# The padding rows of the experts' lists: one DMA of 96 pieces of 512 bytes in place of three of 1024 pieces of 16 bytes

## The chip, the cores and the metric

The kernel runs on one core of a Trainium2 chip. The metric is device time in microseconds (us), from several executions of the same program; a single execution was also taken with the hardware profiler, and all rows below are from that one. The engines are called PE (TensorE; PEld is its weight load), DVE (VectorE), ACT (ScalarE), POOL (GpSimd) and SP (SyncE, which only issues DMAs); SPq and POOLq are their sequencers.

## What is computed

Two stages. The first is attention in two steps: 32 packed queries `p` of each head attend to the 576 keys and values, and the 576 queries `q` then attend to the 32 packed results. The second sends each of the 8 * 576 = 4608 tokens to one of 8 experts (the one with the largest router logit) and scales the expert's output with the softmax weight of that expert.

```
batch, n_heads, seq, head_dim = (8, 8, 576, 64); n_pack = 32
N, D, E, F = (4608, 512, 8, 1024)
p_packed = sm_attn(p, k, v)
out = sm_attn(q, p_packed, p_packed)
...
x = np.ascontiguousarray(attn_out.transpose(0, 2, 1, 3)).reshape(B * S, H * D)
logits = x @ w_gate + modality_bias[modality_id]
e_idx = np.argmax(logits, axis=1)
...
for e in range(E):
    mask = e_idx == e
    h = np.maximum(x[mask] @ w1[e], 0.0)
    out[mask] = gate_w[mask, None] * (h @ w2[e])
```

## The kernel before

Attention goes batch by batch (8 batches). A batch's `k`, `q` and `v` are loaded by SP, each in a DMA of 1152 KB (`load`, line 234); PE transposes them, ACT copies the transposes out of PSUM; PE makes scores, DVE and ACT make the softmax. `xpart` (three steps a batch) makes the attention's output: PE writes a tile of PSUM (`ps<-bd,a2T`, line 366), ACT copies the tokens' values into `xs` (line 371) and the router's logits into `lt` (line 373). `xs` is one tile, not two, so the first copy of a batch waits until the store of the batch before has read it. `xout` (line 377) stores `xs` with one DMA on SP's queue, 1152 KB, into the scratch tensor `x_scr` in DRAM.

The order of all these steps is written out by hand in a string, `ORDER`, for PE, DVE, ACT and SP; POOL is left to the scheduler, which puts its instructions in order of their readiness. Two batches at a time then go through `routing`: `fold` adds up the logits, `bias_all` (the modality's bias) is added on DVE (`lg`, line 440), the largest logit picks the expert, and sums over tokens (`ones_b`, `negtri`) give each token a row in its expert's list.

The lists lie in one DRAM tensor `lst` of E * R = 8 * 4992 rows of four 32-bit words: R is N + PAD, PAD is 384 rows in front of each expert's part, and the tokens' rows follow. A row holds two row numbers in `x_scr`, the row of the output and the gate weight. A token's row is written with an indirect DMA (`scatter`, line 487; 36 of them, 128 rows each). A padding row has 1 << 20 as its output row, which lies outside the output, so that the store at line 887 leaves it out. Blocks of rows are later read back from `lst` (`fetch`, line 754), the tokens gathered from `x_scr` (line 761), and the experts' two matmuls done on them. Up to 200 us the first expert blocks are interleaved with the last batches of attention; from there on only expert blocks run.

The padding rows are written in `routing_consts`, which POOL reaches after the first transposes (`behind` makes its DMAs wait for a copy on ACT). `pad` is a tile in SBUF with E rows of four words in each of its 128 partitions, all the same; a DMA writes one row of each expert from each partition. Behind it in POOL's queue come two more DMAs, `bias2` (`bias` in the rows) and `mid` (the tokens' modalities), and then the instructions that make `bias_all` (lines 126 to 134). The first scatter waits, among others, for the padding's DMAs. Q is 32, P is 128.

Of the kernel before, what the change touches and what calls it, by code (L numbers as in the profile page):

```python
# [11 lines left out]
I32 = mybir.dt.int32  # L12
# [11 lines left out]
def packed_attn_moe_kernel(  # L24
# [14 lines left out]
    nc = tc.nc  # L39
# [3 lines left out]
    E, _, F = w1.shape  # L43
    P = 128
# [8 lines left out]
    PAD = P3  # L53
    Q = P // 4
# [5 lines left out]
    const = ctx.enter_context(tc.tile_pool(name="const", bufs=1))  # L60
# [5 lines left out]
    lst = dram.tile([E * R, 4], I32, name="lst")  # L66
# [24 lines left out]
    meta = const.tile([P, NT, 4], I32, name="meta")  # L91
    metaf = meta.bitcast(F32)
    nc.gpsimd.memset(meta, 0)
    pad = const.tile([P, E, 4], I32, name="pad")
    nc.gpsimd.memset(pad, 0)
    nc.gpsimd.memset(pad[:, :, 1:2], 1 << 20)
    m1 = const.tile([P, NP, NC], F32, name="m1")
# [7 lines left out]
    def behind(ins):  # L105

        tc.add_manual_dep(getattr(ins, "ins", ins), copied[-1].name, SYNC, reason="after the first loads")

    def routing_consts(pool):
        for z in range(0, PAD, P):  # L110
            behind(nc.gpsimd.dma_start(lst.rearrange("(e r) w -> r e w", e=E)[z:z + P], pad))
        mid_d = mod_id.bitcast(I32).rearrange("(i p c w) -> p i (c w)", i=NP, c=NC, w=2)
        mid = sm.tile([P, NP, NC, 2], I32, name="mid", bufs=1)
        bias2 = sm.tile([P, 2, E], F32, name="bias2", bufs=1)
        behind(nc.gpsimd.dma_start(bias2, mod_bias[None].broadcast_to([P, 2, E])))
        behind(nc.gpsimd.dma_start(mid.rearrange("p i c w -> p i (c w)"), mid_d))
        mrow = meta.rearrange("p (i c) w -> p i c w", i=NP)
        for z in range(2):
            nc.gpsimd.iota(mrow[:, :, 5 * z:5 + 4 * z, 1], pattern=[[2 * S, NP], [2, 5 - z]], base=z,
                           channel_multiplier=NC)  # L120
        for z in range(2):
            for u in range(2):
                nc.gpsimd.iota(mrow[64 * u:64 * u + 64, :, :, 3 * z], pattern=[[4 * S, NP], [1, NC]],
                               base=(2 * u + z) * S, channel_multiplier=NC)
        for z in range(2):
            nc.gpsimd.tensor_copy(out=m1[:, :, 5 * z:5 + 4 * z], in_=mid[:, :, z::2, 0])
        m1v = m1.rearrange("p i c -> p (i c)")[:, :, None]
        nc.gpsimd.tensor_scalar(out=m0, in0=m1v, scalar1=-1.0, scalar2=1.0, op0=ALU.mult, op1=ALU.add)
        bias_t = pool.tile([P, NT, E], F32, name="bias_t")
        nc.gpsimd.tensor_tensor(out=bias_all, in0=m0.broadcast_to([P, NT, E]),  # L130
                                in1=bias2[:, 0:1, :].broadcast_to([P, NT, E]), op=ALU.mult)
        nc.gpsimd.tensor_tensor(out=bias_t, in0=m1v.broadcast_to([P, NT, E]),
                                in1=bias2[:, 1:2, :].broadcast_to([P, NT, E]), op=ALU.mult)
        nc.gpsimd.tensor_tensor(out=bias_all, in0=bias_all, in1=bias_t, op=ALU.add)
# [776 lines left out]
    with ExitStack() as actx:  # L911
# [10 lines left out]
        def rest():  # L922
            for m in (4, 8, 12):
                for _ in prep_p(ZL["ps1"], m):
                    pass
                yield
            routing_consts(pzp)
            yield
# [260 lines left out]
```

## Time and profile before

| what | us |
|---|---|
| median of three runs (601.05 to 602.62) | 601.27 |
| the profiled execution, its own time | 601.6 |
| span of the profiled execution, first to last instruction | 599.9 |
| PE busy in it | 558.3 (93%) |
| DVE busy in it | 339.8 (57%) |
| ACT, POOL busy in it | 213.6, 211.0 |

The page cuts the span into 40 slices of 15 us and gives each engine's busy share in tenths. A row of the timeline has the start, the time, the engine, the line, the operation with what it writes and reads, and in brackets how long the engine stood idle before it and which instruction or DMA ended that. A row of the stretches has, for each engine, busy us and the number of instructions, then the granted clock of PE (1.00 is 2.4 GHz, 0.50 is 1.2 GHz), the mean busy share of the 16 DMA engines and what they moved. A DMA's row on an engine is the time of its issue, not of its transfer.

### The profile page before, as it was taken

Reading aid. Unit: us, or ns where it says so; the run is one execution under the profiler, and the core shown is the slowest. Engines: PE = TensorE matmul, PEld = TensorE weight load, DVE = VectorE, ACT = ScalarE, POOL = GpSimd, SP = SyncE. Lnnn points to the kernel's source line nnn. Section 1 sums busy time; section 2 is a strip of 40 time slices with the busy share of each in tenths; the row PEclk is TensorE's granted clock in tenths of the full one; section 3 lists DMA queues with packets and bytes.
Section 4 is the critical chain, followed back from the end, with each engine's and each line's share of the span. In section 5 each row is a group of like instructions: output and inputs, shape, how many; then the busy total and the mean of one; then the engine's idle time right before and its main releaser. Section 6 shows DMA issues by size and latency. Waiting matters only on the chain. (4 is left out here: it accounts for less than half of the span.)

```text
span 599.9 us, 12863 instructions
## 1 busy us (share of the span) xinstructions
PE 558.3 (93%) x4792; PEld 485.4 (81%) x4792; DVE 339.8 (57%) x785; ACT 213.6 (36%) x402; POOL 211.0 (35%) x259
## 2 busy tenths in 40 slices
PE   5999598867799999999999999999999999999994
PEld 4777476745597988988989889898989889989893
DVE  1399497739698717662763436746165375743540
ACT  2587486517443112212213122541222225422230
POOL 4002103651345453445133423164422512741331
PEclk9899799778599999999999999999999999999998
DMA  9799998737233861114551211445211201011331
GB/s 296 240 354 222 348 320 322 222 79 246 91 115 99 194 212 30 61 55 90 141 196 45 70 47 54 99 117 177 74 40 41 86 20 54 37 56 36 54 56 43
DMA packets 33705, 77.09 MB, mean 128 GB/s; under 512 B 7008, under 2 KB 7088, under 8 KB 32576
## 3 DMA queue, kind: packets, MB, share of 16 engines
q1 hardware_dynamic: 24224, 54.92, 29.7%
q0 software_dynamic: 8848, 20.75, 12.3%
q8 instruction: 52, 0.85, 0.6%
q14 instruction: 53, 0.43, 0.3%
q10 hardware_dynamic: 528, 0.13, 0.1%
HBM read 56.53 MB, written 19.26 MB: 126 GB/s over the span
## 5 line engine op out<-in xcount | busy, mean ns | idle before, releaser
L873 PE MATMUL ps_o<-rawq,rawk 128*128 128x512 f32 x460 | 146.8, 390 | 0.0
L837 PE MATMUL ps_h<-x_wide,w1h 128*128 128x256 f32 (+1 forms) x704 | 142.7, 298 | 0.8 <-issue 0.7
L795 DVE STREAM_TRANSPOSE xt<-xt 32x256 f32<-32x256 f32 (+1 forms) x240 | 111.1, 463 | 29.7 <-DMA xt<-x_scr,mt 25.8
L837 PEld LDWEIGHTS ps_h<-x_wide,w1h 128*128 128x128 f32 x704 | 115.0, 189 | 3.3 <-issue 1.7
L761 POOL DMA_INDIRECT xt<-x_scr,mt x82 | 80.6, 983 | 98.5 <-DVE xt L795 30.8
L837 PE MATMUL ps_h<-x_wide,w1l 128*128 128x256 f32 (+1 forms) x352 | 105.3, 299 | 0.7 <-issue 0.7
L873 PEld LDWEIGHTS ps_o<-rawq,rawk 128*128 128x128 f32 x460 | 86.3, 188 | 17.6
L887 POOL DMA_INDIRECT out_dram<-ot,mt x37 | 38.6, 1043 | 122.9 <-ACT ot L879 91.3
L842 DVE SCALAR_TENSOR_TENSOR rawk<-ps_h,rawk 128x256 fp32r<-128x256 f32 (+1 forms) x66 | 29.3, 459 | 86.1 <-ACT rawk L841 72.2
L879 ACT ACTIVATE ot<-ps_o,mt 128x512 f32<-128x512 f32 x35 | 24.1, 689 | 125.6 <-PE ps_o L873 87.9
L837 PEld LDWEIGHTS ps_h<-x_wide,w1l 128*128 128x128 f32 x352 | 66.4, 189 | 0.2 <-issue 0.2
L818 PE MATMUL ps_h<-x_hl,w1h 128*128 128x256 f32 x320 | 58.3, 283 | 1.1 <-issue 1.0
L487 POOL DMA_INDIRECT lst<-meta,dsi x36 | 36.5, 1015 | 52.6 <-DVE nb L268 31.2
L873 PE MATMUL ps_o<-qT,rawk 128*128 128x512 f32 x140 | 54.7, 391 | 0.0
L841 ACT ACTIVATE rawk<-ps_h 128x256 fp32r<-128x256 f32 (+1 forms) x66 | 26.3, 414 | 78.6 <-PE ps_h L837 70.4
L818 PEld LDWEIGHTS ps_h<-x_hl,w1h 128*128 128x128 f32 x320 | 50.0, 189 | 2.0 <-issue 1.5
L818 PE MATMUL ps_h<-x_hl,w1l 128*128 128x256 f32 x160 | 45.3, 284 | 0.1
L299 PE MATMUL ps<-rawv,a1T 64*64 64x128 f32 x576 | 28.4, 308 | 8.8 <-issue 7.1
L873 PE MATMUL ps_o<-rawv,rawk 128*128 128x512 f32 x90 | 35.0, 389 | 0.0
L873 PE MATMUL ps_o<-rawq,x_hl 128*128 128x512 f32 x100 | 34.9, 390 | 0.0
L299 PEld LDWEIGHTS ps<-rawv,a1T 64*64 64x64 f32 x576 | 21.4, 152 | 15.6 <-issue 12.3
L754 POOL DMA_DIRECT2D mt<-lst x19 | 14.9, 782 | 52.3 <-DMA out_dram<-ot,mt 23.8
(234 smaller groups left out, 832.0 us busy)
## 6 DMA issues: line engine op xcount, KB each, us to landing
rawq<-in_q_dram SPq DMA_DIRECT2D x8, 1152.0 KB
rawv<-in_v_dram SPq DMA_DIRECT2D x8, 1152.0 KB
x_scr<-xs SPq DMA_DIRECT2D x8, 1152.0 KB
raw<-in_moe_w_dram SPq DMA_DIRECT2D x32, 256.0 KB
rawk<-in_k_dram SPq DMA_DIRECT2D x7, 1152.0 KB
kT<-in_moe_w_dram SPq DMA_DIRECT2D x4, 1024.0 KB
qT<-in_moe_w_dram SPq DMA_DIRECT2D x3, 1024.0 KB
xt<-x_scr,mt POOLq DMA_INDIRECT x82
```

What stands on the lines that cost most here:

```text
L299: nc.tensor.matmul(pp[u][os_, 0:P], a1T[rs, c, os_], v_t[rs, 2 * pr:2 * pr + 2, TOK[c], :], start=(c == 0), stop=(c == NC - 1), skip_group ...
L487: ins = ins_of(nc.gpsimd.indirect_dma_start(out=lst, out_offset=bass.IndirectOffsetOnAxis(ap=dsi[:, c:c + 1], axis=0), in_=meta[:, i * NC ...
L754: ins = free(nc.gpsimd.dma_start(mt[:, t:], lst[ds(off, rows), :].rearrange("(t p) w -> p t w", p=P)))
L761: return [free(nc.gpsimd.indirect_dma_start(out=xt[:, (t + 2) % 3, u * HW:u * HW + HW], out_offset=None, in_=x_scr[0:NA[ph] * 4 * S] if ph ...
L795: nc.vector.transpose(out=x[w:w + Q, :, z:z + Q], in_=g[z:z + Q, :, w:w + Q])
L818: nc.tensor.matmul(ps[:, f], M[a][:, j, (f0 + f) * P:(f0 + f) * P + P], M["x"][:, j, b, 0:P2], start=(n == 0), stop=(n == 3 * KD - 1))
L837: nc.tensor.matmul(ps, M[a][:, j, f * P:f * P + P], M["x"][:, j, b, cs], start=(n == 0), stop=(n == 3 * KD - 1))
L841: ia = nc.scalar.activation(out=hh, in_=ps, func=AF.Relu)
L842: iv = nc.vector.scalar_tensor_tensor(out=hl, in0=ps, scalar=0.0, in1=hh.bitcast(F32), op0=ALU.max, op1=ALU.subtract)
L873: nc.tensor.matmul(op, hid(M, a, j, 1, slice(t * P, t * P + P))[:, 0], M[b][j // 4][:, j % 4], start=(n == 0), stop=(n == 3 * KF - 1))
L879: ia = nc.scalar.activation(out=ot, in_=op, func=AF.Copy, scale=mt.bitcast(F32)[:, (t + 1) % 3, 2:3])
L887: nc.gpsimd.indirect_dma_start(out=out, out_offset=bass.IndirectOffsetOnAxis(ap=mt[:, (t + 1) % 3, 1:2], axis=0), in_=M["ot"][t == 0], in_ ...
```

## The change

`pad` is made with 12 partitions (PAD // Q) of 32 rows of four words (512 bytes) instead of 128 partitions of 8 rows. One DMA takes the place of the loop of three: from each of the 12 partitions it writes the same 512 bytes to each of the 8 experts, as a run of 32 rows that lie one behind the other in `lst`. What the rows contain, and where they lie, is as before.

```diff
-    pad = const.tile([P, E, 4], I32, name="pad")
+    pad = const.tile([PAD // Q, Q, 4], I32, name="pad")
     nc.gpsimd.memset(pad, 0)
     nc.gpsimd.memset(pad[:, :, 1:2], 1 << 20)
...
     def routing_consts(pool):
-        for z in range(0, PAD, P):
-            behind(nc.gpsimd.dma_start(lst.rearrange("(e r) w -> r e w", e=E)[z:z + P], pad))
+        behind(nc.gpsimd.dma_start(
+            lst.rearrange("(e r) w -> e r w", e=E)[:, 0:PAD].rearrange("e (k r) w -> k e (r w)", r=Q),
+            pad.rearrange("k r w -> k (r w)")[:, None].broadcast_to([PAD // Q, E, 4 * Q])))
```

On PE, DVE, ACT and SP the instructions and their order stay the same. The waits for POOL's DMAs name other semaphores of the same ring of eight, since each later DMA of POOL is now two places earlier in the ring. POOL's queue around the padding before, from the load of the router's weights to the constants that need `mid`:

```order
L1007 DMA wgs<-in_moe_w_gate_dram 64x8x8
L111 DMA lst<-pad 128x8x4 x3
L115 DMA bias_879<-in_moe_modality_bias_dram 128x16
L116 DMA mid<-in_moe_modality_id_dram 128x4x18
L126 CAST m_93<-mid 128x4x5
L126 CAST m_93<-mid 128x4x4
```

The same place after the change (all lines below the new statement are one further down):

```order
L1008 DMA wgs<-in_moe_w_gate_dram 64x8x8
L110 DMA lst<-pad 12x8x128
L116 DMA bias_877<-in_moe_modality_bias_dram 128x16
L117 DMA mid<-in_moe_modality_id_dram 128x4x18
L127 CAST m_93<-mid 128x4x5
L127 CAST m_93<-mid 128x4x4
```

Three DMAs of 128 partitions, 8 experts and 4 words became one of 12 partitions, 8 experts and 128 words; nothing else changed its place.

## Rows read from the trace of the kernel before

**Rows 1.** The page's tenths: PE's busy share in 40 slices of 15 us.

```profile
PE   5999598867799999999999999999999999999994
```

**Rows 2.** Stretches of 4 us: engines' busy us, granted clock, DMA share, GB/s.

```profile
52.00:56.00 4.00, 3.71 (x72) 3.02 (x64) 3.85 (x11) 2.46 (x8) 0.00 (x0) 1.00 1.44 83
56.00:60.00 4.00, 4.00 (x103) 2.50 (x87) 3.52 (x7) 1.95 (x4) 0.00 (x0) 1.00 0.60 94
60.00:64.00 4.00, 0.10 (x14) 0.01 (x2) 1.58 (x3) 0.00 (x0) 0.00 (x0) 1.00 0.96 205
64.00:68.00 4.00, 1.06 (x20) 1.07 (x24) 0.51 (x1) 2.19 (x5) 2.67 (x6) 0.61 1.03 391
68.00:72.00 4.00, 4.00 (x30) 3.64 (x23) 2.23 (x5) 2.83 (x7) 0.00 (x0) 0.54 1.08 401
72.00:76.00 4.00, 4.00 (x117) 3.03 (x114) 2.73 (x8) 2.54 (x5) 0.00 (x0) 1.00 1.00 405
```

**Rows 3.** Waits from 50 to 75 us: who, for whom, total, times, longest.

```profile
ACT xs L371 <- DMA x_scr<-xs: 7.9, 1, 7.9
PE ps L366 <- ACT lt L373: 6.8, 1, 6.8
```

**Rows 4.** Timeline, POOL: start, us, instruction, idle before and its releaser.

```profile
47.70 2.71 POOL L111 DMA_DIRECT2D lst<-pad  x3 [21.09 <-ACT kT L247]
50.40 0.57 POOL L115 DMA_DIRECT2D bias<-n_moe_modality_bias_dram  x1
50.96 0.76 POOL L116 DMA_DIRECT2D mid<-in_moe_modality_id_dram  x1
...
64.73 0.36 POOL L126 CAST m<-mid 128x20 f32<-128x20 int32 x2 [13.01 <-DMA mid<-in_moe_modality_id_dram]
...
66.78 0.79 POOL L134 TENSOR_TENSOR bias_all<-bias_all,bias_t 128x288 f32<-128x288 f32 x1
```

**Rows 5.** Timeline of SP's queue, ACT, DVE and PE around the gap.

```profile
51.20 0.34 SPq L377 DMA_DIRECT2D x_scr<-xs  x1
...
58.94 0.93 PE L366 MATMUL ps<-bd,a2T 64*64 64x136 f32 x24
...
65.81 0.80 ACT L371 COPY xs<-ps 128x768 f32<-128x768 f32 x1 [7.86 <-DMA x_scr<-xs]
...
66.94 1.64 PE L366 MATMUL ps<-bd,a2T 64*64 64x136 f32 x24 [6.83 <-ACT lt L373]
...
67.50 0.75 DVE L348 TENSOR_REDUCE dn<-st 128x18 f32<-128x576 f32 x1 [5.85 <-ACT st L345]
...
68.50 3.50 PE L243 MATMUL ps<-ident,rawq 128*128 128x128 f32 x16
...
72.98 0.23 DVE L440 TENSOR_TENSOR lg<-ps,bias_all 128x72 f32<-128x72 f32 x1 [2.54 <-PE ps L436]
...
76.12 1.09 PE L243 MATMUL ps<-ident,rawq 128*128 128x128 f32 x8
```

**Rows 6.** The stores of `xs`: their size (part 6), and a later one's timeline.

```profile
x_scr<-xs SPq DMA_DIRECT2D x8, 1152.0 KB
...
85.83 0.34 SPq L377 DMA_DIRECT2D x_scr<-xs  x1
...
94.42 0.80 ACT L371 COPY xs<-ps 128x768 f32<-128x768 f32 x1 [0.66 <-PE ps L366]
```

**Rows 7.** Later: a stretch, one group of matmuls, waits 100 to 200 us, scatters.

```profile
200.00:595.00 395.00, 389.33 (x2343) 354.11 (x2342) 202.21 (x437) 105.41 (x193) 149.59 (x149) 1.00 0.29 80
...
73.99 2.20 PE L299 MATMUL ps<-rawv,a1T 64*64 64x128 f32 x72
...
PE ps L299 <- issue: 7.1, 14, 1.0
...
PEld ps L299 <- issue: 11.6, 21, 1.2
...
L487 POOL DMA_INDIRECT lst<-meta,dsi x36: 957/974/1693, 98.8 to 267.2; - x36
```

## The prediction

> **What bounds the kernel now.** I read the tenths of the page first: TensorE is at nine tenths from the twelfth of 40 slices to the last but one, its dips lie in the first third, and after the start the deepest is the fifth slice (60 to 75 us) [rows 1]. From 200 us on it is busy 389.3 of 395.0 us [rows 7], so DMA traffic can give nothing there; but a gain before 200 us moves that whole block forward and is kept. So the question is what the attention stage waits for where this change acts.
>
> The table of stretches shows it. DMA moves 391 to 405 GB/s from 64 to 76 us, but 83 GB/s in 52 to 56 and 94 GB/s in 56 to 60, and in 60 to 64 TensorE works 0.10 us of 4 [rows 2]. The waits name what the engines see: ScalarE's copy of `xs` stood 7.9 us for the DMA `x_scr<-xs`, and TensorE 6.8 us for ScalarE [rows 3]. The timeline gives the order [rows 4, 5]: GpSimd issues the three list-padding DMAs at 47.70 (2.71 us for three), then `bias` at 50.40 and `mid` at 50.96; SyncE issues the first `x_scr<-xs` at 51.20; ScalarE is free at 57.95 (65.81 - 7.86) and starts its next `xs` copy only at 65.81, because `xs` is one buffer that the store still reads; and `mid`, behind the padding in GpSimd's queue, releases its first reader at 64.73, 13.0 us after its issue ended. So what stands behind the padding in its own queue and a store in another queue at the same time are both late by many microseconds, while few bytes move. That is what 3072 pieces of 16 bytes would do, 192 to each of 16 DMA engines. From the end of the first padding DMA's issue (47.70 + 0.9 = 48.6) to 64.73 are 16.1 us, so a piece took at most about 84 ns (an estimate, an upper bound).
>
> **The change part by part.**
>
> 1. *Three DMAs become one.* GpSimd issues for 0.9 us instead of 2.71 [rows 4]. It then idles 13.0 us for `mid` anyway, so these 1.8 us are worth nothing by themselves. The two fills of `pad` stay two fills at the start, smaller: nothing.
>
> 2. *96 pieces of 512 bytes instead of 3072 of 16.* The bytes are the same 48 KB. The trace has no piece of 512 bytes with a price, so I bound it: below by its bytes at the full rate (405 GB/s over 16 engines is 25 GB/s each: 20 ns), above by a small piece plus its bytes (84 + 20 = 104 ns). Six pieces an engine are 0.1 to 0.6 us, against up to 16 before. Either end is far below what follows, so the choice does not matter.
>
> On how they spread there is a rule that speaks against the new form. `pad` now has 12 partitions, and the order of GpSimd's queue, shown with the change, has a DMA of 12 by 8 by 128 words. The Trainium skill, "DMA: Bandwidth & Descriptors", section "Rules for kernel authors", says to put a dimension that is a multiple of 16 outermost, since an outermost size below 16 confines the DMA to at most that many engines; by it 12 engines would carry 8 pieces each and 4 none. No row of this trace has such a DMA.
>
> 3. *The store `x_scr<-xs` at 51.20.* It is 1152 KB [rows 6]. At 391 to 405 GB/s that is 2.9 to 3.0 us after an issue that ends at 51.5: it could land at about 54.5. The other end: the store issued at 85.83 had landed by 94.42, when ScalarE wrote `xs` again and had waited for TensorE, not for the DMA [rows 6]: 8.6 us at most, 59.8 here. ScalarE is free at 57.95, so its wait falls from 7.86 us to between 0 and 1.9. I take 0, because a small rest is covered. TensorE starts its `ps<-bd,a2T` matmuls 1.13 us after the `xs` copy starts (66.94 against 65.81) and is itself busy until 60.11 (66.94 - 6.83): 1.0 us of a rest is hidden. VectorE's `dn` starts 1.69 us after the copy (67.50) and VectorE is busy until 61.65 (67.50 - 5.85): 2.0 us are hidden [rows 5]. At the far end TensorE loses 0.9.
>
> 4. *What comes forward.* TensorE's 6.83 us of idling go. Behind them the granted clock is 0.61 and 0.54 in the stretches 64 to 72, so most of that is at 1.2 GHz instead of 2.4 [rows 2]: the 24 matmuls take 1.64 us where the same group took 0.93 at 58.94, and 16 transposes take 3.50 us where 8 take 1.09 at 76.12 (some 2.1 for 16) [rows 5]. Without the idling I expect the full clock: 0.7 + 1.4 = 2.1 us. TensorE comes forward by 6.83 + 2.1 = 8.9 us. VectorE comes forward by the 5.85 us that it waited for the exponential. The router's logits then reach it at 72.98 - 8.9 = 64.1, before it asks for them (72.98 - 2.54 - 5.85 = 64.6), so the 2.54 us that it waited for them go too: 8.4 us. The least of the two counts: **8.4 us**. If the clock stayed low, the logits would come at 66.15 and VectorE would gain 5.85 + 1.0 = 6.8.
>
> 5. *What is late next.* The q, k and v loads queued behind the store on SyncE's queue run at about 400 GB/s from 64 us to 76. They come forward with the store: store and first q load are 2.36 MB or 5.9 us, so q is there at 58 to 59, and TensorE asks for it at 61. The constants that hang on `mid` are needed by the logits at 64.6 instead of 72.98; they took 2.8 us after `mid` landed (67.57 against 64.73) [rows 4], and `mid` is no longer behind 3072 pieces. The later waits are released by engines or by DMAs that are issued after 64 us, so they move along.
>
> The profiled execution took 601.6 us, with a span of 599.9. 601.6 - 8.4 = 593.2, and the median of the three runs is 0.3 below the profiled one: **592.9 us**.
>
> **The rivals.**
>
> *The new DMA still holds the store.* If the 96 pieces went through one DMA engine, that engine would need 2 to 10 us for them, and its share of the store would end between 56.5 and 64.5. In the middle (60.5) ScalarE waits 2.5 us, TensorE loses 1.5 and VectorE 0.5; TensorE's gain is then the least, 7.4 us: 593.9. At the bad end the wait is 6.5, TensorE loses 5.5 of 8.9 and the time is 597.9. On 12 engines, 8 pieces each are at most 0.8 us, which is hidden as in step 3. By the skill's rule above, the time is thus that of the forecast. For it: an outer size of 12 where the neighbours in the queue have 64 and 128. Against: the pieces lie in 12 partitions, not in one.
>
> *The padding is not what held the store.* `mid` (512 pieces of 72 bytes) and `bias` share the stretch. Then the stall stays: 601.3 us. Against it: `mid` itself is late, which something ahead of it has to explain. Here belongs too that the DMA is cut into 16-byte pieces after all.
>
> *Slower: TensorE runs dry beside the scatters.* 72 matmuls of `ps<-rawv,a1T` take 2.20 us at 73.99, where nothing is scattered. Where GpSimd writes the tokens into the lists (36 scatters, the first at 98.8) the same line has 14 gaps without a releaser, 7.1 us on TensorE and 11.6 us at its weight loads, over two such groups [rows 7]. The cause is not in the trace. If TensorE, which gains 8.9 us where VectorE gains 8.4, met more of the scatters, a third group would cost 3.6 to 5.8 us (half of either sum): 596.5 to 598.7. It is slower than before by over 0.3% only from 8.4 + 1.8 = 10.2 us of new gaps, nearly twice what there is now: 603.1 us or more. For it: the gaps are large and not understood. Against: scatters and matmuls are released from one chain and come forward together.
>
> **How the numbers follow.** Forecast, 590 to 596 (a gain of 5.9 to 8.9 us, and one stretch of low clock, 2.1 us, more or less further on): 0.62. More, below 590, if the later gaps shrink: 0.08. Part lost, 596 to 599.5 (one DMA engine, or a third group of gaps): 0.14. No change, 599.5 to 603.1 (the padding is not the cause): 0.10. Slower, above 603.1: 0.06. About 0.3% (1.8 us) is what a measurement of this kernel can tell from no change; so faster 0.84, same 0.10, slower 0.06. The range from 588 to 598.5 holds the forecast's band, most of the stronger case and most of the weaker one.
>
> **What would show it right or wrong.** Right: no wait of the `xs` copy for `x_scr<-xs`; DMA near 400 GB/s in most of 52 to 60; TensorE busy at full clock from 60 to 68; `mid` released some 5 us after its issue; the first scatter at about 90.4 instead of 98.8. Step 3 is wrong if the `xs` copy still waits over 2 us; step 4 if the first scatter comes forward by much less than 8 us though that wait is gone; step 5 if a wait for q, k, v or `mid` appears before 76 us, or if the time from the first scatter to the end of the span grows.

## The result, and the profile after

| | before | after |
|---|---|---|
| median of six runs each, us | 601.16 | 590.08 |
| range, us | 598.18 to 603.58 | 588.56 to 592.38 |
| profiled execution, span, us | 599.9 | 587.0 |

The ratio is 0.984 with a 95% interval of 0.9807 to 0.9874: a gain of 7.6 to 11.6 us. The medians differ by 11.1 us. (The ratios, here and below, are those given with the measurement; they differ a little from the quotients of the medians, 0.982 here.) The 8.4 us of the forecast lie inside that interval, near its lower end. The profiled execution of after is the fastest of its six (588.56 us), so the two traces lie 13.0 us apart, 2.0 more than the medians.

The stretches of after, with the columns of [rows 2] (busy us of PE, PEld, DVE, ACT, POOL, then the granted clock, DMA share and GB/s):

```profile
52.00:56.00 4.00, 3.62 (x64) 2.91 (x61) 3.85 (x12) 2.44 (x8) 1.87 (x5) 1.00 1.01 316
56.00:60.00 4.00, 4.00 (x87) 2.36 (x84) 3.67 (x7) 3.77 (x8) 1.39 (x2) 1.00 1.01 389
60.00:64.00 4.00, 4.00 (x80) 3.53 (x84) 3.72 (x8) 3.79 (x9) 0.00 (x0) 1.00 1.05 397
64.00:68.00 4.00, 4.00 (x108) 2.93 (x102) 3.80 (x11) 2.73 (x6) 0.00 (x0) 1.00 1.03 412
68.00:72.00 4.00, 4.00 (x50) 3.37 (x48) 3.79 (x13) 3.13 (x5) 0.00 (x0) 1.00 1.04 397
```

The DMA engines now move 316 and 389 GB/s where they moved 83 and 94, PE works 4.00 us of the 4 in which it had worked 0.10, and the granted clock, which fell to 0.61 and 0.54 behind the gap, stays at 1.00.

The timeline of POOL, then SP's queue, ACT, PE and DVE around the place of [rows 4, 5]:

```profile
47.68 0.66 POOL L110 DMA_DIRECT2D lst<-pad  x1 [21.09 <-ACT kT L248]
...
54.03 0.56 POOL L127 CAST m<-mid 128x20 f32<-128x20 int32 x2 [4.31 <-DMA mid<-in_moe_modality_id_dram]
...
90.45 1.13 POOL L488 DMA_INDIRECT lst<-meta,dsi  x1 [32.98 <-ACT lt L374]
...
51.17 0.34 SPq L378 DMA_DIRECT2D x_scr<-xs  x1
...
58.40 0.80 ACT L372 COPY xs<-ps 128x768 f32<-128x768 f32 x1 [0.23 <-ACT kT L248]
...
60.24 0.93 PE L367 MATMUL ps<-bd,a2T 64*64 64x136 f32 x24
61.12 1.97 PE L244 MATMUL ps<-ident,rawq 128*128 128x128 f32 x16
...
61.64 0.75 DVE L349 TENSOR_REDUCE dn<-st 128x18 f32<-128x576 f32 x1
...
64.50 0.19 DVE L441 TENSOR_TENSOR lg<-ps,bias_all 128x72 f32<-128x72 f32 x1
```

Against [rows 5]: the `xs` copy starts at 58.40 instead of 65.81 and has no wait for the store; the matmuls and the transposes behind it run at the full clock (0.93 and 1.97 us for what took 1.64 and 3.50) without a gap; `dn` and `lg` have no idle time ahead of them. The first scatter stands at 90.45 instead of 98.8.

How the gain runs on is seen at a group of the experts' second matmuls (a tile's instructions: duration, then first and last start) and at the last store of the output (timeline). The matmuls of before:

```profile
L873 PE MATMUL ps_o<-rawq,rawk x460: 387/389/477, 206.3 to 590.2; 128*128 128x512 f32 x154
```

The same group of after:

```profile
L874 PE MATMUL ps_o<-rawq,rawk x460: 387/389/476, 196.7 to 579.1; 128*128 128x512 f32 x154
```

The last store of before:

```profile
595.18 1.00 POOL L887 DMA_INDIRECT out_dram<-ot,mt  x1 [6.57 <-POOLq L1150]
```

And of after:

```profile
582.62 1.00 POOL L888 DMA_INDIRECT out_dram<-ot,mt  x1 [5.14 <-POOLq L1151]
```

The lead in these two traces is 8.3 us at the first scatter, 9.6 at 206 us, 11.1 at 590 and 12.6 at the last store.

**Where the cost is recorded.** The DMA view of before from 51 to 65 us (queue, packets, MB, share of the 16 engines' time):

```profile
DMA packets 718, 2.22 MB, mean 159 GB/s; under 512 B 111, under 2 KB 175, under 8 KB 588
...
q1 hardware_dynamic: 556, 2.09, 93.9%
q0 software_dynamic: 160, 0.09, 5.5%
```

The same view of after from 51 to 57 us:

```profile
DMA packets 532, 1.92 MB, mean 321 GB/s; under 512 B 84, under 2 KB 100, under 8 KB 403
...
q1 hardware_dynamic: 435, 1.81, 91.4%
q0 software_dynamic: 96, 0.09, 5.3%
```

q0 is GpSimd's queue with the padding, `bias` and `mid`; q1 carries the store and the loads. The padding does not look guilty: its queue fills 5.5% and 5.3% of the engines' time. The time stands in the records of the other queue, 93.9% for 2.09 MB in 14 us where after needs 91.4% for 1.81 MB in 6. "The DMA engines are 94% busy" says nothing of who holds them; the GB/s beside it shows that they are held. A piece has no record of its own: counted by size in the trace, the padding of before is 48 of q0's 160 packets, 1024 bytes or 64 pieces each, that of after 12 of its 96, 4096 bytes or 8 pieces each. The numbers of pieces below are those of the DMAs' shapes.

### The profile page after: what moved, and what is told of

Same layout as the page of the kernel before. It is cut to its first block, busy times and chain, and to the rows that moved or that the text cites. A ratio compares the mean times of both kernels' runs of the same rounds, so it can differ in the third digit from the quotient of the medians.

```text
span 587.0 us, 12860 instructions
## 1 busy us (share of the span) xinstructions
PE 550.7 (94%) x4792; PEld 478.2 (81%) x4792; DVE 339.7 (58%) x785; ACT 212.7 (36%) x402; POOL 209.2 (36%) x257
## 3 DMA queue, kind: packets, MB, share of 16 engines
q0 software_dynamic: 8784, 20.75, 12.6%
## 5 line engine op out<-in xcount | busy, mean ns | idle before, releaser
L300 PE MATMUL ps<-rawv,a1T 64*64 64x128 f32 x576 | 27.5, 284 | 11.7 <-issue 9.2
L300 PEld LDWEIGHTS ps<-rawv,a1T 64*64 64x64 f32 x576 | 19.9, 138 | 19.4 <-issue 15.1
```

Source lines behind the costliest of these rows:

```text
L300: nc.tensor.matmul(pp[u][os_, 0:P], a1T[rs, c, os_], v_t[rs, 2 * pr:2 * pr + 2, TOK[c], :], start=(c == 0), stop=(c == NC - 1), skip_group ...
```

## The experiments

The runs fell on chips of two kinds: before takes 598 to 601 us on one (the comparison above, the two rows marked 598, and secondxs and earlypad further down) and 575 us on the other. Every ratio is against before on the same chip, with its 95% interval.

| kernel | pieces beside `mid`'s and `bias`'s | first padding issue to first reader of `mid`, us | store's issue to next `xs` copy, us (its wait for the store) | ratio |
|---|---|---|---|---|
| before | 3072 of 16 B | 17.0 | 14.6 (7.9) | |
| after | 96 of 512 B | 6.4 | 7.2 (none) | 0.984 |
| before, 575 us | 3072 of 16 B | 15.7 | 13.3 (6.5) | |
| after, 575 us | 96 of 512 B | 6.1 | (none) | 0.9889 |
| three512 | 96 of 512 B, 3 DMAs | 6.5 | (none) | 0.9894 |
| three512b | the same again | 6.2 | (none) | 0.9902 |
| pieces48 | 1024 of 48 B | 8.8 | 7.6 (0.8) | 0.9898 |
| mixed16 | 1024 of 16 B, 64 of 512 B | 8.4 | 7.6 (0.8) | 0.9922 |
| double16 | 6144 of 16 B | 25.5 | 19.4 (12.4) | 1.015 |
| putback16 (598) | 96 of 512 B, 3072 of 16 B | 19.2 | 15.2 (7.2) | 1.0103 |
| sbuf16 (598) | the same, the 3072 into SBUF | 12.2 | 8.1 (1.4) | 0.9938 |

### Pieces, bytes or DMAs

Three DMAs of 4 partitions by 8 pieces of 512 bytes:

```diff
-        behind(nc.gpsimd.dma_start(
...
+        for z in range(0, PAD // Q, 4):
+            behind(nc.gpsimd.dma_start(
+                lst.rearrange("(e r) w -> e r w", e=E)[:, 0:PAD].rearrange("e (k r) w -> k e (r w)", r=Q)[z:z + 4],
+                pad.rearrange("k r w -> k (r w)")[z:z + 4, None].broadcast_to([4, E, 4 * Q])))
```

> Three DMAs again, but of 32 pieces of 512 bytes each, from 4 partitions each. Theory A (number of small pieces): no wait of the xs copy for the store, 590 us as the changed kernel. Rival B (each DMA costs, or the 1.8 us of issue on GpSimd matter): the wait of 7.9 us is back and the time is 601. Rival C (few engines): 4 partitions could go through 4 DMA engines with 8 pieces each; still no wait.

1024 pieces of 48 bytes (the same bytes, from 128 partitions, in one DMA):

```diff
+    PQ = 3
-    pad = const.tile([PAD // Q, Q, 4], I32, name="pad")
+    pad = const.tile([PAD // PQ, PQ, 4], I32, name="pad")
...
-            lst.rearrange("(e r) w -> e r w", e=E)[:, 0:PAD].rearrange("e (k r) w -> k e (r w)", r=Q),
+            lst.rearrange("(e r) w -> e r w", e=E)[:, 0:PAD].rearrange("e (k r) w -> k e (r w)", r=PQ),
```

> The padding in one DMA of 1024 pieces of 48 bytes from 128 partitions (a third of the pieces of before, the same bytes). Theory A, the store is held by the number of small pieces: in the traces 3072 pieces held it by 65.3 - 56.4 = 9 us, so 1024 hold it by about 3 us; it lands at 59 to 60, the xs copy waits 1 to 2.5 us, TensorE loses 0 to 1.5 us, and the time is 590 to 592. Rival B, the cost is a fixed one for each DMA (three against one): the xs copy waits for nothing and the time is that of the changed kernel, 590.

The first third of the padding in the old form, the rest in the new one:

```diff
+        behind(nc.gpsimd.dma_start(lst.rearrange("(e r) w -> r e w", e=E)[0:P], pad0))
...
-            lst.rearrange("(e r) w -> e r w", e=E)[:, 0:PAD].rearrange("e (k r) w -> k e (r w)", r=Q),
+            lst.rearrange("(e r) w -> e r w", e=E)[:, P:PAD].rearrange("e (k r) w -> k e (r w)", r=Q),
```

> The first 128 padding rows of each expert in one DMA of 1024 pieces of 16 bytes, the other 256 rows in one of 64 pieces of 512 bytes. Theory A (number of small pieces): like 1024 pieces of 48 bytes, the xs copy waits 1 to 2.5 us, 590 to 592 us. Rival B (each DMA costs): two DMAs, half of the stall, 4 us of wait, 594 to 596.

Measured: 569.71, 569.75 and 570.37 us beside 575.09; ratios 0.9894 [0.986, 0.9927], 0.9898 [0.9868, 0.9927] and 0.9922 [0.989, 0.9954]. How long the padding took from issue to landing is the last number in the rows of the DMA issues (KB each, us to landing). three512:

```profile
lst<-pad POOLq DMA_DIRECT2D x3, 16.0 KB, 4.9
```

mixed16, the third in the old form:

```profile
lst<-pad POOLq DMA_DIRECT2D x1, 16.0 KB, 7.6
```

Before, on another 575 us chip (its run is further down):

```profile
lst<-pad POOLq DMA_DIRECT2D x3, 16.0 KB, 11.7
```

And after, on that chip:

```profile
lst<-pad POOLq DMA_DIRECT2D x1, 48.0 KB, 5.0
```

Three DMAs of 512-byte pieces land as soon as one does, so the number of DMAs is not it. All forms write the same 48 KB, and 1024 pieces delay `mid` about alike with all of it (8.8 us) and with 16 KB of it in them (8.4), so the bytes are not it either: the number of small pieces is. No run had many pieces of 512 bytes, so what is due to their number and what to their being small is not separated. A thousand of them are nearly free here: `xs` waits 0.8 us, a little under the 1 to 2.5 us expected and less than the 1.0 and 2.0 us that step 3 had found hidden on PE and DVE, and the three times differ by less than their intervals.

### The 16-byte pieces put back

After, with three DMAs of 1024 pieces into a DRAM tile that nobody reads; then the same number into SBUF; then before with 3072 more into DRAM:

```diff
+            behind(nc.gpsimd.dma_start(dst16[z:z + P, :, 0:4], src16))
```

> The changed kernel with three more DMAs of 1024 pieces of 16 bytes each right behind the new one, from SBUF into a DRAM tensor that nobody reads. Theory A (number of small pieces): the stall of before is back, the xs copy waits 7 to 8 us, mid is late by 8 to 9 us, 600 to 602 us. Rival E, the stall hung on the lists' own addresses (the padding rows lie in eight blocks): no wait, 590.

```diff
+        for z in range(3):
+            behind(nc.gpsimd.dma_start(d16[:, z, :, 0:4], s16))
```

> The changed kernel with three more DMAs of 1024 pieces of 16 bytes each right behind the new one, but from SBUF to SBUF (into the tile for the weights, which is free until 130 us). Theory A in its plain form, every piece costs a DMA engine its time wherever it goes: the stall is back, the xs copy waits 7 to 8 us, 600 to 602 us. Theory A2, it is small writes to DRAM that cost the time: the xs copy waits less than 2 us and the time is 590 to 592.

```diff
         for z in range(0, PAD, P):
             behind(nc.gpsimd.dma_start(lst.rearrange("(e r) w -> r e w", e=E)[z:z + P], pad))
+        for z in range(0, PAD, P):
+            behind(nc.gpsimd.dma_start(dst16[z:z + P, :, 0:4], src16))
```

> The kernel before with 3072 more pieces of 16 bytes, in three more DMAs from another tile to a DRAM tile that nobody reads. Theory (each piece takes its time on the 16 DMA engines; from the first padding issue to the first reader of mid it was 17.0 us with 3072 pieces and 6.4 with 96, so 10.7 us for 3072): mid is released about 27.7 us after the first padding issue, the xs copy waits about 7.9 + 10.7 = 18.6 us, and the time is 10 to 13 us above before. Rival (the stall is a fixed time of a DMA that runs beside the store, or of the write to lst itself, which later readers and the scatters depend on): the wait of the xs copy stays near 8 us and the time near that of before.

The timeline's rows of the `xs` copy and of `mid`'s first reader in putback16:

```profile
65.21 0.80 ACT L377 COPY xs<-ps 128x768 f32<-128x768 f32 x1 [7.24 <-DMA x_scr<-xs]
...
65.75 0.36 POOL L132 CAST m<-mid 128x20 f32<-128x20 int32 x2 [14.58 <-DMA mid<-in_moe_modality_id_dram]
```

In sbuf16:

```profile
60.41 0.80 ACT L376 COPY xs<-ps 128x768 f32<-128x768 f32 x1 [1.35 <-DMA x_scr<-xs]
...
60.99 0.36 POOL L131 CAST m<-mid 128x20 f32<-128x20 int32 x2 [7.57 <-DMA mid<-in_moe_modality_id_dram]
```

In double16:

```profile
69.45 0.80 ACT L376 COPY xs<-ps 128x768 f32<-128x768 f32 x1 [12.44 <-DMA x_scr<-xs]
...
72.01 0.36 POOL L131 CAST m<-mid 128x20 f32<-128x20 int32 x2 [18.84 <-DMA mid<-in_moe_modality_id_dram]
```

putback16 brings the wait of the copy back with data that has nothing to do with the lists, and no gain is left: 601.88 beside 597.87 us, 1.0103 [1.006, 1.0146]. (PE waits 4.6 us behind it, where it waited 5.5 to 6.8 in the two traces of before.) That it is above before, by 4.0 us in the medians, is not explained; its profiled execution was the fastest of four (598.16 to 603.69), and the first scatter stands there at 98.80 us, where it stood in the trace of before (98.78).

double16 gives the price. With 96, 3072 and 6144 small pieces, `mid` comes 6.1, 15.7 and 25.5 us after the first padding issue, all on the same chip: 9.6 and 9.8 us for each 3072. Spread evenly, these are 192 on each of 16 DMA engines, so the price is an estimate of 50 ns a piece and engine (56 on the first pair: 17.03 - 6.35 over 192). `mid`, in the same queue, feels all of it. The store does not: the copy's wait for it grew by 5.9 us, not by the 10.7 expected, and from the store's issue to the next copy it took 13.3 and then 19.4 us. That the store gets a share of the engines while the padding lasts would explain this; it is argued, not shown. The time rose by 9.1 us, to 584.08, 1.015 [1.0101, 1.0199], where 10 to 13 were expected. The first scatter moved back by 5.7 us (96.98 to 102.66), as the wait did; the rest of the 9.1 is not explained, but the interval, 5.8 to 11.4 us, begins close to the 5.7.

sbuf16 changes only where the pieces go: beside the 6.4 us of after, pieces of the same size into SBUF delay `mid` by 5.9 us where those into DRAM (putback16, the same chip) delay it by 12.9. In both, `mid`'s own issue ends 2.6 us later, since GpSimd issues three more DMAs ahead of it; counted from there, its reader waits 7.57 and 14.58 us where it waited 4.31 in after. The `xs` copy waits 1.4 us instead of 7.2. So most of the cost is in the small writes to DRAM. The time is 593.24 us, 0.9938 [0.9912, 0.9964], a little above the 590 to 592 expected; after was not run on that chip. The Trainium skill, "DMA: Bandwidth & Descriptors", section "Why small descriptors are slow (HBM only)", says that transfers inside SBUF don't pay the price of small descriptors; the traces agree in part, since 3072 such pieces still keep `mid` in their own queue waiting 3.3 us longer (7.57 against 4.31).

### Who is hit by the stall

`bias` and `mid` issued ahead of the padding (based on before):

```diff
-        for z in range(0, PAD, P):
-            behind(nc.gpsimd.dma_start(lst.rearrange("(e r) w -> r e w", e=E)[z:z + P], pad))
...
+        for z in range(0, PAD, P):
+            behind(nc.gpsimd.dma_start(lst.rearrange("(e r) w -> r e w", e=E)[z:z + P], pad))
```

> The kernel before, with bias and mid issued ahead of the three padding DMAs instead of behind them. Theory A: mid lands some 4 us after its issue, since nothing is ahead of it, but the store is held as before, the xs copy waits 7 to 8 us and the time is 601. Rival D, the store was held by mid's 512 pieces of 72 bytes: they now run earlier, so the store is held less and the time is 590 to 596.

A second buffer for `xs`, so that the copy need not wait (based on before):

```diff
+            if b == 1 and "xs" not in D_:
+                D_["xs"] = W["raw1"][:, 0:NC * 2 * P].rearrange(
+                    "p (c r d) -> p c r d", c=NC, r=2)
```

> The kernel before, but the second batch's xs lies in another, free tile, so that its copies need not wait for the first store. Theory A: the wait for x_scr<-xs is gone, but the loads behind the store in SyncE's queue are held with it: q lands at 65.7 as before, TensorE asks for it at 61 and waits 4 to 5 us; the gain is 2.5 to 5 us, 596 to 599 us. Rival F, only the one xs buffer made the held store expensive: the whole gain, 590.

The padding issued some 21 us earlier, behind the load of the router's weights (based on before):

```diff
+                        for z_ in range(0, PAD, P):
+                            behind(nc.gpsimd.dma_start(lst.rearrange("(e r) w -> r e w", e=E)[z_:z_ + P], pad))
```

> The kernel before, with the three padding DMAs of 16-byte pieces issued at 26 us, right behind the router's weights, where DMA is idle for some 4 us. Theory A (every transfer beside the small pieces is held): the loads of v and k issued at 27.4 and 28.0 are held by up to 9 us, TensorE waits for k at 34 to 42 us, the store at 51 is free; the time is 592 to 601. Rival G, only the store (a write to DRAM) is held by other writes, loads are not: no wait, 590.

The timeline of midfirst, `mid`'s first reader and the `xs` copy:

```profile
56.55 0.36 POOL L126 CAST m<-mid 128x20 f32<-128x20 int32 x2 [4.55 <-DMA mid<-in_moe_modality_id_dram]
...
65.25 0.80 ACT L371 COPY xs<-ps 128x768 f32<-128x768 f32 x1 [6.54 <-DMA x_scr<-xs]
```

The timeline of secondxs, ACT's copy (into the second buffer, a part of the tile `raw1`), SP's issue of the load of q, and PE's use of it:

```profile
59.40 0.80 ACT L374 COPY raw<-ps 128x768 f32<-128x768 f32 x1 [0.24 <-PE ps L366]
...
52.84 0.38 SPq L234 DMA_DIRECT2D rawq<-in_q_dram  x1
...
66.22 3.26 PE L243 MATMUL ps<-ident,rawq 128*128 128x128 f32 x16 [3.84 <-DVE a2T L356]
```

A wait of earlypad, 26 to 50 us:

```profile
PE ps L297 <- DMA rawv<-in_v_dram: 6.6, 1, 6.6
```

And two stretches of it, with the columns of [rows 2]:

```profile
36.00:40.00 4.00, 1.57 (x25) 0.97 (x9) 3.75 (x11) 3.58 (x8) 0.00 (x0) 1.00 0.86 48
40.00:44.00 4.00, 0.00 (x0) 0.00 (x0) 0.00 (x0) 0.00 (x0) 0.00 (x0) 0.57 0.81 260
```

midfirst frees `mid` early (4.55 us of wait instead of 11.7 to 13.0) and changes nothing for the better: the store still holds the copy 6.54 us (7 to 8 were expected, and in before on the other 575 us chip it is 6.5); 577.29 beside 575.09, 1.0033 [1.0001, 1.0065]. So `mid` was late but not missed.

secondxs takes the copy's wait away and gains nothing in the time: 598.06 beside 597.87, 1.001 [0.998, 1.0039], where 2.5 to 5 us were expected. PE now stands 3.84 us before the transposes of q instead. The profile puts that down to `a2T` on DVE, but in before the same transposes started at 68.50 [rows 5] while that `a2T` started only afterwards:

```profile
69.66 0.78 DVE L356 STREAM_TRANSPOSE a2T<-st 128x576 f32<-128x576 f32 x1
```

So they don't depend on it. What is left, by elimination, is q itself, issued at 52.84 behind the store in the same queue. The wait for `xs` was the first of two that ended at nearly the same time, 14.6 us behind the store's issue in before and 13.8 here. The first scatter of secondxs stands 48.0 us behind the padding's issue, 3.1 us less than in the trace of before; why nothing of that is left in the time stays open.

earlypad shows that the padding carries its stall with it: no wait of the `xs` copy for the store, but PE waits 6.6 us for v (not for k, as expected), at 48 GB/s from 36 to 40 us and with the clock at 0.57 behind it; 600.57 beside 597.87, 1.0068 [1.0037, 1.01].

### Before and after on another chip

> The kernel before, unchanged, so that its trace stands beside the traces of the same chip. Both theories: ScalarE's xs copy waits about 7.9 us for x_scr<-xs and the first scatter stands about 98.8 us after the start. If the gaps without a releaser at the weight loads of ps<-rawv,a1T (21 gaps, 11.6 us in the first trace of before; hardly any in the traces of the chip on which before takes 575 us) belong to the chip and not to the kernel, they are here when before takes about 600 us and absent when it takes about 575.

> The changed kernel, unchanged. Theory A (the stall of 8.4 us is the whole of the gain, and what came on top of it in the first comparison, 11.1 us in the medians, is the scatter of the later low clock): the first scatter comes 8 to 9 us earlier than in the trace of before on the same chip, and the medians differ by 6 to 9 us. Rival B (2.5 us more are systematic, because the later work falls better): the medians differ by 10.5 to 12 us again. On a chip where before takes about 575 us, A expects about 0.989, as for the 96 pieces in three DMAs (0.9894).

> 96 pieces of 512 bytes as in the changed kernel, but in three DMAs of 4 by 8 pieces. Theory (the number of pieces decides): within 0.3% of the changed kernel on the same chip, no wait of the xs copy for the store. Rival (the number of DMAs, or of partitions that they read, decides): the wait is back in part, 2 to 8 us, and the time 2 to 8 us above the changed kernel.

before took 575.01 us there, after 568.87: 0.9889 [0.9859, 0.9919], 6.1 us in the medians. three512b took 569.3: 0.9902 [0.9868, 0.9936], the same as after. The waits of before there from 45 to 95 us:

```profile
ACT xs L371 <- DMA x_scr<-xs: 6.5, 1, 6.5
...
PE ps L366 <- ACT lt L373: 5.5, 1, 5.5
DVE dn L348 <- ACT st L345: 4.7, 1, 4.7
DVE lg L440 <- PE ps L436: 3.1, 1, 3.1
```

The group of `ps_o` matmuls that was shown above, in before:

```profile
L873 PE MATMUL ps_o<-rawq,rawk x460: 387/389/477, 185.1 to 564.6; 128*128 128x512 f32 x154
```

And in after:

```profile
L874 PE MATMUL ps_o<-rawq,rawk x460: 387/389/476, 177.0 to 556.4; 128*128 128x512 f32 x154
```

The first scatter of before:

```profile
96.98 1.12 POOL L487 DMA_INDIRECT lst<-meta,dsi  x1 [31.81 <-DVE nb L268]
```

And of after:

```profile
89.20 1.12 POOL L488 DMA_INDIRECT lst<-meta,dsi  x1 [34.09 <-ACT st L346]
```

The lead is 7.8 us at the first scatter (8 to 9 were expected), 8.1 at 185 and 8.2 at 565: next to nothing is added on the way. 1.1 of it is the start, since GpSimd reaches the padding at 45.54 in after and at 46.61 in before; 6.7 to 7.1 are left for a stall of the copy of 6.5. DVE's two waits there are 7.8 us. Neither the copy's wait nor the first scatter of before is what was expected of it there (7.9 and 98.8 us): the stall is shorter on that chip.

## Why the prediction was right, step by step

*Step 1, GpSimd's issue time is worth nothing: right.* It issues for 0.66 us instead of 2.71, and three512b, which issues for 1.83 us, has the time of after on the same chip.

*Step 2, the price of the pieces: right as a bound.* 50 to 56 ns a 16-byte piece, below the 84 ns taken as the most; the 3072 pieces are some 10 us, not 16, since the 16.1 us also held what `mid` takes in any case (4.3 us in after). By the rule of the Trainium skill that the prediction cites ("DMA: Bandwidth & Descriptors", section "Rules for kernel authors"), an outer size of 12 leaves 4 of 16 engines without a piece. The trace agrees as far as its records go: the padding of after is 12 packets of 4096 bytes and 4 of 32. What that costs was not tested, since three512 has 12 such packets too and no run has 96 pieces on more; it lands as soon (4.9 us against 5.0), and in neither does the copy wait for the store.

*Step 3, the copy's wait falls to 0: right.* 0.23 us, and that for ACT itself. When the store lands is not read from this row, only that it has landed by 58.17 us (58.40 - 0.23).

*Step 4, 8.4 us: right at the place for which it was worked out.* The first scatter came forward by 8.3 us, PE's clock stays at 1.00 from 60 to 72 us, and the transposes take 1.97 us where 2.1 was the estimate (twice 1.09 is nearer to 2.2, which changes nothing, since VectorE's 8.4 is the least). On the other chip its recipe (the least of what PE and DVE gain) starts from DVE's 4.7 + 3.1 = 7.8 us, and 6.7 to 7.1 came in the traces, 6.1 in the medians.

*Step 5, nothing else late: right.* PE takes q at 61.12 without a wait, and `mid` was released 4.3 us after its issue (5 were expected). The time from the first scatter to the end of the span did not grow either (501.1 us before, 496.5 after). secondxs shows that this step was needed: with the loads behind the store still late, taking the copy's wait away changes nothing in the time.

*The total: 2.7 us short of the medians.* The forecast moved everything behind 72 us along, and its band allowed for 2.1 us more or less of low clock further on. In the first pair of traces 2.8 us more came between the first scatter (8.3) and 590 us (11.1). Of these, 1.3 had come by 206 us; PE's clock was 0.86 from 135 to 200 us before and 0.95 after. The other 1.5 came among the expert blocks, where the clock is 1.00 in both. On the other chip next to nothing came on top (7.8, then 8.1 and 8.2), and the medians there differ by less than the lead. So no run shows that the extra belongs to the change, and its cause stays open: executions of one kernel lie 4 to 5 us apart, and the comparison was not made again on a chip of the first kind. What the runs bear out is the 8.4 us up to the first scatter; that the whole stayed within the 590 to 596 us of the forecast (590.08) is in part luck.

*The rivals.* That the new DMA still holds the store would have kept a wait of over 2 us; there is none. That the padding was not the cause falls with putback16, double16 and earlypad. PE's dry stretches beside the scatters did grow, but by 4.2 us where 10.2 were needed to lose the gain (waits without a releaser from 95 to 200 us of after, against 7.1 and 11.6 in [rows 7]):

```profile
PEld ps L300 <- issue: 13.7, 19, 1.9
...
PE ps L300 <- issue: 9.2, 19, 1.6
```

PE's overlap with those of its weight load, so the real loss is nearer to 2 us (7.1 to 9.2 on PE alone).

## What to carry to other kernels

Count the pieces of a DMA that writes to DRAM, not only its bytes: 48 KB in 3072 pieces of 16 bytes held a store in another queue by 6 to 8 us and its own queue by 10, while 1024 pieces were hidden and 96 of 512 bytes left no wait. Such a DMA was found here where GB/s collapse (83 to 205) while the DMA engines' busy share stays high (0.60 to 1.44), and the wait is named by somebody else's transfer. Taking away the wait that the profile names (secondxs) or moving the DMA (earlypad) handed the stall on here, because other transfers were queued beside or behind it.

## What the runs showed of the hardware that was not expected

The same program takes 600 us on some chips and 575 on others, and most of the 25 us arise in one stretch: the first `ps_o` matmul of the group above starts at 206.3 us in the one trace of before and at 185.1 in the other, the first scatters at 98.78 and 96.98. The matmuls of `ps<-rawv,a1T` differ (groups by line: busy us, mean ns, idle before them and what ended it). In the first trace of before:

```profile
L299 PE MATMUL ps<-rawv,a1T 64*64 64x128 f32 x576 | 28.4, 308 | 8.8 <-issue 7.1 <-DVE lg L440 1.4
```

In before on the 575 us chip:

```profile
L299 PE MATMUL ps<-rawv,a1T 64*64 64x128 f32 x576 | 20.1, 287 | 1.3 <-DVE lg L440 1.3
```

The gaps without a releaser beside the scatters are 8.7 to 13.7 us at the weight loads in all six traces from chips of the 600 us kind, and at most 1.1 us in all eight from chips of the 575 us kind, with nearly the same instructions. So they go with the chip, or with something on it that the trace doesn't show; the prediction had counted them as a risk of the kernel. They are not all of the 21 us: in the two groups above PE's idle time differs by 7.5 us and its busy time by 8.3, and the granted clock from 95 to 200 us was 0.84 in the one and 0.95 in the other. What they are stays open.
